# Hash products on four 32-column strips of the array, and normalised rows on ScalarE

## The chip, the cores and the metric

One core of a Trainium2 chip runs one program. The metric is the device time of one execution in microseconds; a run gives several executions and the median is quoted. One execution more is taken with the hardware profiler on, and the views below are all of that one.

## What is computed

Three layers run one after the other on 2 x 768 tokens of width 512. The first is attention with 8 heads of width 64 in which a query sees only the keys of its own hash bucket; the bucket is the sign pattern of six projections. The second mixes tokens by the real part of a two-dimensional Fourier transform, normalises each row and applies a feed-forward of width 2048. The third is a gated layer of width 1024.

```python
q_bits = (np.einsum('bhsd,dk->bhsk', q, proj) > 0)      # proj is 64 x 6; k_bits likewise
mask = q_bucket[:, :, :, None] == k_bucket[:, :, None, :]
scores = np.where(mask, scale * q @ k.T, -1e9)          # then softmax, then @ v
...
u = x + np.real(fft(fft(x, axis=1), axis=2))
un = (u - mu) / np.sqrt(var + 1e-06)                    # mu, var of each row of 512
y = u + np.maximum(un @ w_ch1, 0.0) @ w_ch2
...                                                     # gated layer: w_in, gelu, w_sg, w_out
```

## The kernel before, in words

**Tiling.** Attention is cut into 16 heads (2 batches of 8), two heads to a group (8 groups), and each head into 6 items of 128 queries. An item is a 128 x 768 score tile `s` on TensorE (L394), its row maximum on VectorE (L404), the exponential on ScalarE (L406), a split into high and low halves (L251 on ScalarE or L253 on GpSimd, then L258 on GpSimd), a transpose by DMA (L445), and the product with V (L462 to L464).

**The hash.** `prep_group` loads the two `x` tiles of a group; each has the 64 query rows over the 64 key rows, 768 tokens wide. For each half of the tokens (384) and each of the two heads one matmul in F32 (L311) multiplies `x` by `zp`, 128 x 24, so `z` holds 24 rows of projections, 6 for queries and 6 for keys of each head. One ScalarE instruction turns `z` into signs, `bits` (24 rows x 768 columns, F16, L280, in `to_bits`). For each head `prep_head` multiplies `bits` by a table of codes in two matmuls of 384 columns (L360) and `one_hot` writes the result behind the query and key rows (L287, L289). Scores of unlike buckets come out low in the score product itself. The first group's hash is at the head of the program; the others are spread over the items before their heads.

**The normalisation.** After the Fourier steps of a batch (`fft`), `norm` makes for each of 6 row blocks `un = (u - mu) * i` in F32 on VectorE (L640), a high half on ScalarE (L641), a low half on GpSimd (L642) and a transpose by DMA (L643), which gives `unT`, the operand of the feed-forward. In batch 0 the tiles `un` and `hl` share a ring of four buffers of the tag `k2` with the first feed-forward tiles. In batch 1 `un` has one buffer.

**What sets the order.** The program is written as merged streams: attention, weight decoding (the int64 view of the float64 weights is turned to F32 at L226 to L228, then split at L239 and L241), Fourier and feed-forward. Then `Order`, a list scheduler with a table of costs, plans all of it and fixes the order on each engine and of the DMA issues on SP. It plans several times: a rank that blends the start time of the best plan so far with the tail of each node, one plan for each entry of `BLEND`, and keeps the plan with the shortest planned time. Each engine then runs its instructions strictly in that order.

**The stages.** Items of batch 0 until about 143 us; Fourier of batch 0 between the items of batch 1; first feed-forward matmuls (L667, L688) at 232.5 us; the rest of batch 1's attention until 367 us under the feed-forward of batch 0; Fourier of batch 1; feed-forward of batch 1 until 546 us; the gated layer (L764, L787, L804) until the end.

Of the kernel before, what the change touches and what calls it, by code (L numbers as in the profile page):

```python
# [81 lines left out]


def _until(gen, cond):
    for _ in gen:
        if cond():
            return
# [16 lines left out]
class Kern:  # L104
    def __init__(self, tc, I, out):
        self.tc, self.nc, self.I, self.out = tc, tc.nc, I, out
        self.W = {}
        self.c2n, self.att_over = 0, False


# [43 lines left out]
    def setup(self, ctx):  # L154
# [122 lines left out]

    def to_bits(self, out, z):
        if BITS == "A":
            self.nc.scalar.activation(out, z, AF.Sign, bias=self.tiny[0:24])  # L280
        else:
            self.nc.vector.tensor_scalar(out=out, in0=z, scalar1=0.0, scalar2=None, op0=ALU.is_gt)

    def one_hot(self, eng, qo, ko, c):
# [8 lines left out]
    def prep_group(self, ap, vp, n, G):  # L293
# [10 lines left out]
        yield  # L304
        bits = self.bits[n % 2]
        to = bits[0:24].rearrange("p (a c) -> p a c", a=2)
        z = None if ZP[b] else self.ps.tile([P, 2, 512], F32, tag="s", name="z")
        for hf in range(2):
            zh = self.pp.tile([P, 512], F32, tag="p", name="z")[:, 0:HS] if ZP[b] else z[:, hf, 0:HS]
            for hl in range(GH):  # L310
                nc.tensor.matmul(zh[0:24], self.zp[:, hl, :], xs[hl][:, hf * HS:(hf + 1) * HS], start=hl == 0, stop=hl == GH - 1)  # L311
            if ZP[b]:
                self.to_bits(to[:, hf], zh[0:24])
        if not ZP[b]:
            self.to_bits(to, z[0:24, :, 0:HS])
        yield
# [23 lines left out]
    def prep_head(self, ap, n, hl, G):  # L340

        nc, I = self.nc, self.I
        b, g = divmod(n, NG)
        eng = ENG0 if n + hl == 0 else ENG[b]
        x = G["x"][hl]
        if GH * n + hl in FULL:
            q1, k1 = (ap.tile([P, S], F32, tag=nm, name=nm, bufs=SB) for nm in ("q1", "k1"))
            nc.sync.dma_start(out=q1[0:64], in_=I["qk"][b, GH * g + hl, 0:64])
            self.copy(eng["hi"], k1[0:64], x[64:128], SCALE)
            G[hl] = ((q1, k1),)  # L350
        else:
            G[hl] = self.stacks(ap, x, eng)
            q1, k1 = G[hl][0]
        yield
        bits = self.bits[n % 2]
        qo, ko = (y[64:128].rearrange("p (a c) -> p a c", a=2) for y in (q1, k1))
        ct = None if CP[b] else self.ps.tile([P, 2, 512], F32, tag="s", name="ct")
        for hf in range(2):
            c = self.pp.tile([P, 512], F32, tag="p", name="ct")[:, 0:HS] if CP[b] else ct[:, hf, 0:HS]
            nc.tensor.matmul(c, self.codes[:, hl, :], bits[:, hf * HS:(hf + 1) * HS], start=True, stop=True)  # L360
            if CP[b]:
                self.one_hot(eng["oh"], qo[:, hf], ko[:, hf], c)
        if not CP[b]:
            self.one_hot(eng["oh"], qo, ko, ct[:, :, 0:HS])
        yield
# [248 lines left out]
    def norm(self, fp, up, b, unT, mv, ts):  # L614
# [13 lines left out]
        nc.vector.reciprocal(s, i)  # L628
        nc.vector.tensor_tensor(out=self.tok[b][:, 2 * t0:2 * t0 + w], in0=rs, in1=s, op=ALU.mult)
        yield 0.9  # L630
        for t in ts:
# [5 lines left out]
            for n, X in enumerate((A, Bt)):  # L637
                un = fp.tile([P, DM], F32, tag="k2" if LN1[b] else "un", name="un", bufs=4 if LN1[b] else 1)
                hl = fp.tile([P, 2, DM], F16, tag="k2" if LN1[b] else "hl", name="hl", bufs=4 if LN1[b] else 2)
                nc.vector.tensor_scalar(out=un, in0=X, scalar1=mv[:, t, n, 0:1], scalar2=i[:, 2 * (t - t0) + n:2 * (t - t0) + n + 1], op0=ALU.subtract, op1=ALU.mult)  # L640
# [184 lines left out]
    def g_weights(self, wp):  # L825
# [7 lines left out]
        for nm, n, c in (("in", 4, 1024), ("out", 2, 1024), ("sg", 6, 768)):  # L833
            rs[nm] = [wp.tile([P, c], F32, tag=f"{nm}{j}", name=f"{nm}{j}") for j in range(n)]
            spare = sp["sg"] if nm == "sg" else (self.spare if nm == "out" else sp["in"])
            yield from self.weight(wp, nm, I["w_" + nm], rs[nm], spare, c, nc.sync)
        nc.vector.tensor_scalar(out=self.gB, in0=self.gB, scalar1=self.sc["sg"][0], scalar2=None, op0=ALU.mult)
        yield 0.5

    def build(self):  # L840
# [3 lines left out]
        with ExitStack() as ctx:  # L844
# [16 lines left out]
            def prep1():  # L861
                yield from self.weight(w1p, "w1a", I["w1"], r1[1:], r1[0], 1024, nc.sync, (0, 2, 4, 6))

            att = self.attention(ap, (ep0, ep1))
            p1 = prep1()
# [17 lines left out]
            def prep2():  # L883
                for half in HALVES:
                    if half == "b":
                        yield from self.weight(w2p, "w1b", I["w1"], r2[4:8], self.spare, 1024, nc.sync, (1, 3, 5, 7))
                    k = 8 * (half == "b")
                    bl = (4, 5, 6, 7) if k else (0, 1, 2, 3)
                    yield from self.weight(w2p, "w2" + half, I["w2"], r2[k:k + 4], self.spare, 1024, nc.sync, bl)
                    nc.vector.tensor_tensor(out=self.prod[half], in0=self.sc["w1" + half][0], in1=self.sc["w2" + half][0], op=ALU.mult)  # L890
                self.stage += 1

            def main0():
                yield from self.fft(fp0, 0, unT[0])
                self.stage += 1
                yield from self.ch(fp0, 0, unT[0], CH0, (("k2", 4),) * 4 + (("k1", 2),) * 2 + (("k3", 2),) * 2)

            def second():
# [7 lines left out]
                with tc.tile_pool(name="fft1", bufs=1) as fp:  # L906
                    yield from self.fft(fp, 1, unT[1], up)

# [13 lines left out]

            _run(_merge((self.ch(hp, 1, unT[1], CH1), 1.0), (side(), W3)))
            c_r.close()
# [14 lines left out]
class Order:  # L939
# [11 lines left out]
    def __init__(self, tc, room):  # L951
        self.tc, self.room = tc, room
        self.tiles = {t.name: t for t in tc.info.tiles}
# [31 lines left out]
    def cost(self, i, rd, wr):  # L985
# [3 lines left out]
        if e == "PE":  # L989
# [281 lines left out]
    def best(self):  # L1271
        self.rank = list(range(len(self.nodes)))
        self.slots()
        t, order = self.plan()
        found = t, order, [(n.start, n.end) for n in self.nodes]
        begin = [n.start for n in self.nodes]
        for f in self.BLEND:
            tail = self.tails()
            self.rank = [f * x - (1.0 - f) * y for x, y in zip(begin, tail)]
            t, order = self.plan()  # L1280
            if t < found[0]:
                found = t, order, [(n.start, n.end) for n in self.nodes]
                begin = [n.start for n in self.nodes]
        return found[1]

# [17 lines left out]
def _tables():  # L1303
# [21 lines left out]
    rl[0] = np.where(l % 2 == 0, 1.0, -1.0)  # L1325
    codes = np.zeros((P, GH, P), np.float16)
    sign = np.where((np.arange(64)[None, :] >> np.arange(NB)[:, None]) & 1, 1.0, -1.0)
# [4 lines left out]
    pops = np.zeros((P, 2), np.float32)  # L1332
    if BITS == "A":
        pop = np.full_like(pop, NB)
    pops[0:64, 0] = BIG * (1.0 - pop)
# [49 lines left out]
```

## Time and profile before

| | us |
|---|---|
| median of 3 runs | 695.46 |
| range of the runs | 695.41 to 697.05 |
| profiled execution | 692.43 |
| its span | 690.6 |
| mean granted clock of TensorE | 0.963 |

The profiled execution lies 3.03 us below the median, and 1.8 us of it lie outside the span. In the rows, PE is TensorE's matmuls, PEld its weight loads, DVE VectorE, ACT ScalarE, POOL GpSimd, SP the issuer of the DMAs. `L311` is line 311 of the kernel. A matmul's shown duration includes its way through the array, so the distance between two starts, not the duration, is what one costs in a full stream. An FP32 matmul stands as two records.

### The profile page before, as it was taken

What the parts mean: (1) busy time and instruction counts of PE and PEld (TensorE: products, weight loads), DVE (VectorE), ACT (ScalarE), POOL (GpSimd) and SP (SyncE); (2) the same over time, 40 slices, a digit from 0 to 9 for tenths busy, and PEclk for the clock granted to TensorE, in tenths of its full rate; (3) what the DMA queues carried; (4) which work ended last, traced back from release to release, by engine and by line L of the source; (5) the groups of instructions that cost most, each with busy time, mean ns of one, the idle gap of its engine ahead of it and who ended that gap; (6) DMA issues with size and microseconds to landing.
All of it is one profiled execution on the core that took longest, in us unless ns stands there. A gap on an engine that the chain in (4) does not pass through costs nothing.

```text
span 690.6 us, 12566 instructions
## 1 busy us (share of the span) xinstructions
PE 627.7 (91%) x4832; PEld 416.9 (60%) x4832; DVE 503.2 (73%) x1137; ACT 347.8 (50%) x540; POOL 232.3 (34%) x197
## 2 busy tenths in 40 slices
PE   4899988865986689999999999998999999999997
PEld 2586776844664467667777658666766444444443
DVE  7968675599799987889557289858563467876663
ACT  5899797866577574467442222324632143322100
POOL 3576645596477630445345032000000022111000
PEclk9999999985996799999999999999999999999999
DMA  8999979999999995786563025943000031211334
GB/s 325 265 163 198 202 176 201 199 245 279 249 209 232 225 220 174 184 184 115 108 107 110 1 36 122 257 126 103 31 1 0 1 58 36 32 31 31 67 86 122
DMA packets 184204, 95.19 MB, mean 138 GB/s; under 512 B 166544, under 2 KB 167312, under 8 KB 183632
## 3 DMA queue, kind: packets, MB, share of 16 engines
q1 hardware_dynamic: 183568, 94.25, 61.3%
q8 instruction: 38, 0.62, 0.4%
q10 hardware_dynamic: 576, 0.14, 0.1%
q14 instruction: 22, 0.18, 0.1%
HBM read 39.31 MB, written 3.15 MB: 61 GB/s over the span
## 4 chain that ended last, share of the span: by engine, by line
PE 44%; DVE 10%; DMA 5%; ACT 2%; POOL 1%; issue 1%; DVEq 0%; POOLq 0%; ACTq 0%
PE c L667 10%; PE c L688 9%; PE gi L764 9%; PE sg L787 7%; PE go L804 5%; DMA wide<-w_in 3%; DMA wide<-w 1%; PE y L549 1%; PE s L394 1%; DVE xu L692 1%; DVE w L241 1%; DVE h L676 1%; DVE nm L404 1%; DVE in L227 1%; DVE w L227 1%
## 5 line engine op out<-in xcount | busy, mean ns | idle before, releaser
L258 POOL TENSOR_TENSOR eh<-e,eh 128x768 f16<-128x768 f32 x80 | 138.5, 1735 | 103.1 <-ACT eh L251 100.8
L667 PE MATMUL c<-unT,w 128*128 128x256 f16 x1152 | 137.2, 277 | 4.8 <-DVE h L676 4.1
L688 PE MATMUL c<-w,h 128*128 128x512 f16 x576 | 131.7, 379 | 1.7 <-DVE xu L692 1.7
L667 PEld LDWEIGHTS <-w 128*128 128x128 f16 x1152 | 113.5, 99 | 27.9 <-issue 7.4
L394 PE MATMUL s<-k,q 128*128 128x384 f32 x384 | 100.1, 391 | 31.4 <-ACT e L406 18.2
L404 DVE TENSOR_REDUCE nm<-s 128x1 f32<-128x768 f32 x96 | 90.2, 949 | 32.7 <-PE s L394 31.4
L406 ACT ACTIVATE e<-s,nm 128x768 f32<-128x768 f32 x96 | 85.2, 896 | 40.2 <-DVE nm L404 28.1
L394 PEld LDWEIGHTS s<-k,q 128*128 128x128 f32 x384 | 69.4, 205 | 41.0 <-ACT e L406 21.7
L688 PEld LDWEIGHTS <-h 128*128 128x128 f16 x576 | 55.5, 98 | 60.9 <-issue 2.6
L780 POOL TENSOR_TENSOR vh<-gv,vh 128x512 f16<-128x512 f32 x12 | 13.9, 1156 | 195.5 <-ACT vh L779 195.5
L675 ACT ACTIVATE h<-c 128x256 f16<-128x256 f32 x96 | 35.0, 377 | 60.4 <-PE c L667 59.9
L676 DVE SCALAR_TENSOR_TENSOR h<-c,h 128x256 f16<-128x256 f32 x96 | 39.1, 418 | 34.3 <-ACT h L675 34.3
L462 PE MATMUL pav<-V,et 128*128 128x65 f16 x480 | 55.3, 199 | 7.4 <-DVE xu L471 4.1
L462 PEld LDWEIGHTS <-et 128*128 128x128 f16 x480 | 46.6, 103 | 16.4 <-issue 10.6
L463 PE MATMUL pav<-V,et 128*128 128x64 f16 x480 | 54.9, 198 | 0.0
L464 PE MATMUL pav<-V,et 128*128 128x65 f16 x480 | 54.8, 200 | 0.0
L764 PE MATMUL gi<-in,xT 128*128 128x512 f16 x216 | 50.5, 379 | 0.0
L764 PEld LDWEIGHTS <-xT 128*128 128x128 f16 x288 | 28.1, 98 | 35.0 <-issue 1.1
L463 PEld LDWEIGHTS <-et 128*128 128x128 f16 x480 | 46.6, 101 | 1.9 <-issue 0.7
L464 PEld LDWEIGHTS <-et 128*128 128x128 f16 x480 | 46.5, 101 | 0.0
L253 POOL TENSOR_SCALAR eh<-e 128x768 f16<-128x768 f32 x32 | 32.7, 1022 | 32.2 <-ACT e L406 25.6
L251 ACT ACTIVATE eh<-e 128x768 f16<-128x768 f32 x48 | 40.3, 839 | 3.0 <-DMA et<-eh 2.5
(221 smaller groups left out, 999.4 us busy)
## 6 DMA issues: line engine op xcount, KB each, us to landing
wide<-w SPq DMA_DIRECT2D x24, 512.0 KB, 4.5
x<-qk SPq DMA_DIRECT2D x16, 384.0 KB, 4.8
k<-q SPq DMA_DIRECT2D x28, 192.0 KB, 3.6
wide<-w SPq DMA_DIRECT2D x4, 1024.0 KB, 9.0
wide<-w_in SPq DMA_DIRECT2D x16, 256.0 KB, 3.1
vst<-v SPq DMA_DIRECT2D x8, 396.0 KB, 6.0
y<-ot SPq DMA_DIRECT2D x12, 256.0 KB, 2.3
q<-q SPq DMA_DIRECT2D x14, 192.0 KB, 4.5
```

Source lines behind the costliest of these rows:

```text
L258: (self.nc.vector if eng == "D" else self.nc.gpsimd).tensor_tensor(out=out, in0=a, in1=b, op=ALU.subtract)
L394: nc.tensor.matmul(s[:, hf, 0:HS], q[:, qs], k[:, hf * HS:(hf + 1) * HS], start=n == 0, stop=n == len(pairs) - 1)
L404: nc.vector.tensor_reduce(nm, x["s"], axis=AX.XY, op=ALU.max, negate=True)
L406: nc.scalar.activation(e.rearrange("p (a c) -> p a c", a=2), x["s"], AF.Exp, bias=nm)
L462: nc.tensor.matmul(pv[:, qt, 0:65], et[:, kb, :], V[:, hl, kb, 64:129], start=kb == 0, stop=False)
L463: nc.tensor.matmul(pv[:, qt, 0:64], et[:, kb, :], V[:, hl, kb, 0:64], start=False, stop=False)
L464: nc.tensor.matmul(pv[:, qt, 0:65], et[:, NT + kb, :], V[:, hl, kb, 64:129], start=False, stop=kb == NT - 1)
L667: nc.tensor.matmul(ps[:, 0:step], w1[kc][:, a, fo], uT[:, 4 * u + kc, o * P:o * P + step], start=m == 0, stop=m == 11)
L676: nc.vector.scalar_tensor_tensor(out=hh[:, 1, :], in0=ps[:, 0:step], scalar=0.0, in1=hh[:, 0, :], op0=ALU.max, op1=ALU.subtract)
L688: nc.tensor.matmul(ps, hs[n, half, f][:, a, j * P:(j + 1) * P], wv[:, w, :], start=f + m == 0, stop=f == NF - 1 and m == 2)
L764: nc.tensor.matmul(ps, xT[:, 4 * a + kc, :], w_in[kc][:, w, half * DM:(half + 1) * DM], start=n == 0, stop=n == 11)
L787: nc.tensor.matmul(ps, w_sg[kt][:, w, t * P:(t + 1) * P], vh[b][:, kt, a, :], start=n == 0, stop=n == 17)
```

## The change

- **Hash products.** The 768 tokens are cut in four quarters of 192. `zp` gets 32 columns for each head in place of 24. For each head and quarter one matmul of 192 columns goes to a strip of 32 columns of the array, so that `z` is 128 rows by 192 columns in place of 24 by 768. The sign instruction reads and writes 128 x 192.
- **Codes.** Since the signs of quarter g lie on rows 32g to 32g + 23, the table of codes stands four times, once for each strip, the other rows zero. It is zeroed by GpSimd and filled by four DMAs from ScalarE's queue, where one was. The product with the codes is four matmuls of 192 columns for each head. The zeroing of the two `bits` tiles goes.
- **Rows.** `un` is made on ScalarE as `i * u + g` with `g = -mu * i`; `g` is one small VectorE instruction more in each call of `norm` (one call in batch 0, three in batch 1).
- **Order.** The planner prices an F32 matmul with 32 output rows at a quarter, blends with 0.75 six times in place of five different values, and shifts the rank of the stream that loads and decodes `w_out` by -15 us. Naming of the streams is only for that.

```diff
+UN = ('A', 'A')
-BITS = 'A'
+SQ = S // 4
...
-        self.codes = cp.tile([P, GH, P], F16, tag="codes", name="codes")
+        self.codes = cp.tile([P, 4, GH, P], F16, tag="codes", name="codes")
+        nc.gpsimd.memset(self.codes, 0.0)
...
-        nc.scalar.dma_start(out=self.codes, in_=I["codes"])
+        for g in range(4):
+            nc.scalar.dma_start(out=self.codes[32 * g:32 * g + 2 * GH * NB, g], in_=I["codes"])
...
-        self.zp = cp.tile([P, GH, 2 * GH * NB], F32, tag="zp", name="zp")
+        self.zp = cp.tile([P, GH, 32], F32, tag="zp", name="zp")
...
-            t = cp.tile([P, S], F16, tag=f"bits{i}", name=f"bits{i}")
-            nc.gpsimd.memset(t, 0.0)
+            t = cp.tile([P, SQ], F16, tag=f"bits{i}", name=f"bits{i}")
...
-        for hf in range(2):
-            zh = self.pp.tile([P, 512], F32, tag="p", name="z")[:, 0:HS] if ZP[b] else z[:, hf, 0:HS]
-            for hl in range(GH):
-                nc.tensor.matmul(zh[0:24], self.zp[:, hl, :], xs[hl][:, hf * HS:(hf + 1) * HS], start=hl == 0, stop=hl == GH - 1)
...
-            self.to_bits(to, z[0:24, :, 0:HS])
+            z = self.ps.tile([P, 2, 512], F32, tag="s", name="z")[:, 0, 0:SQ]
+        for hl in range(GH):
+            for c in range(4):
+                nc.tensor.matmul(
+                    z[32 * c:32 * c + 32], self.zp[:, hl], xs[hl][:, c * SQ:(c + 1) * SQ],
+                    start=hl == 0, stop=hl == GH - 1, tile_position=(0, 32 * c),
+                )
+        nc.scalar.activation(self.bits[n % 2], z, AF.Sign, bias=self.tiny)
...
-            nc.tensor.matmul(c, self.codes[:, hl, :], bits[:, hf * HS:(hf + 1) * HS], start=True, stop=True)
+            for a in range(2):
+                nc.tensor.matmul(c[:, a * SQ:(a + 1) * SQ], self.codes[:, 2 * hf + a, hl], bits, start=True, stop=True)
...
+        if UN[b] == "A":
+            g = fp.tile([P, w], F32, tag="lnm", name="lnm", bufs=1 if LN1[b] else 2)
+            nc.vector.scalar_tensor_tensor(
+                out=g.rearrange("p (a c) -> p a c", c=2), in0=mv[:, t0:ts[-1] + 1, :, 0], scalar=-1.0,
+                in1=i.rearrange("p (a c) -> p a c", c=2), op0=ALU.mult, op1=ALU.mult,
+            )
...
+                if UN[b] == "A":
+                    nc.scalar.activation(un, X, AF.Identity, scale=i[:, c], bias=g[:, c])
...
+    SHIFT = {"out": -15.0}
-    BLEND = (0.0, 0.25, 0.5, 0.75, 0.9)
+    BLEND = (0.75,) * 6
...
-                return x * (2 if i.is_transpose else 4) / 2400 + 0.0065
+                return x * (2 if i.is_transpose else 1 if wr[0][2] - wr[0][1] == 32 else 4) / 2400 + 0.0065
...
-            self.rank = [f * x - (1.0 - f) * y for x, y in zip(begin, tail)]
+            self.rank = [f * x - (1.0 - f) * y + z for x, y, z in zip(begin, tail, self.shift)]
```

## Rows read from the trace of the kernel before

**Rows 1.** Stages: busy us of PE, PEld, DVE, ACT, POOL (instructions), granted clock, DMA share.
```profile
34.00:138.00 104.00, 94.92 (x1013) 79.84 (x1012) 70.49 (x111) 90.73 (x123) 64.09 (x51) 0.98 0.99 190
138.00:207.00 69.00, 52.47 (x525) 38.81 (x524) 60.67 (x97) 45.96 (x68) 47.89 (x41) 0.85 1.09 245
207.00:258.00 51.00, 35.71 (x314) 28.11 (x315) 47.61 (x87) 35.68 (x51) 31.45 (x24) 0.77 1.09 227
258.00:690.00 432.00, 422.68 (x2861) 256.22 (x2859) 294.58 (x802) 152.21 (x268) 73.56 (x57) 1.00 0.37 85
546.00:690.00 144.00, 140.02 (x648) 63.23 (x647) 95.74 (x314) 35.10 (x53) 13.88 (x12) 1.00 0.26 55
```

**Rows 2.** Chain that ended last, pieces: start, length in us, what.
```profile
253.49 1.24 DVE w L227
...
262.54 2.69 PE z L311 x8
...
546.75 36.42 PE gi L764 x168
```

**Rows 3.** Groups of instructions: count, busy us, mean ns of one, idle before.
```profile
L311 PE MATMUL z<-x,zp 128*24 128x384 f32 x64 | 23.8, 515 | 7.4 <-DVE zp L172 4.6 <-ACT e L406 1.4 <-DMA x<-qk 1.4
L280 ACT ACTIVATE bits<-z,tiny 24x768 f16<-24x768 f32 x8 | 7.1, 885 | 2.7 <-PE z L311 2.7
L675 ACT ACTIVATE h<-c 128x256 f16<-128x256 f32 x96 | 35.0, 377 | 60.4 <-PE c L667 59.9
```

**Rows 4.** Weight loads of one group's hash products: start, length in us.
```profile
263.13 0.10 PEld L311 LDWEIGHTS z<-x,zp 128*24 128x24 f32 x1 [0.22 <-issue]
263.45 0.10 PEld L311 LDWEIGHTS z<-x,zp 128*24 128x24 f32 x1 [0.22 <-issue]
```

**Rows 5.** Matmuls of lines 463 and 464: start, length in us.
```profile
27.05 0.19 PE L463 MATMUL pav<-V,et 128*128 128x64 f16 x1
27.08 0.20 PE L464 MATMUL pav<-V,et 128*128 128x65 f16 x1
```

**Rows 6.** First 12 us: ScalarE's queue, its first instruction, GpSimd's zeroing.
```profile
1.16 0.46 ACTq L163 DMA_DIRECT2D codes<-codes  x1
...
5.59 0.84 ACT L251 ACTIVATE k<-q 64x768 fp32r<-64x768 f32 x1 [1.69 <-DVE q L255]
...
L176 POOL MEMSET bits<- 128x768 f16 x2 | 1.4, 737 | 0.3 <-POOLq L1373 0.3
```

**Rows 7.** Row normalisation of batch 0 on VectorE, and GpSimd beside it.
```profile
213.08 0.58 DVE L640 TENSOR_SCALAR un<-xu,mv,ln 128x512 f32<-128x512 f32 x1
...
216.89 1.79 DVE L640 TENSOR_SCALAR un<-xu,mv,ln 128x512 f32<-128x512 f32 x1
...
216.74 3.43 POOL L258 TENSOR_TENSOR eh<-e,eh 128x768 f16<-128x768 f32 x2
```

**Rows 8.** Line 640, VectorE's busy us (x instructions), granted clock, in both batches.
```profile
213.00:236.00 23.00, 6.59 (x6) 0.65 1.12 214
396.00:424.00 28.00, 3.27 (x6) 1.00 0.30 48
```

**Rows 9.** ScalarE instructions of 128x512: with a scale by row, without.
```profile
L731 ACT ACTIVATE ghl<-xu,x_i 128x512 f16<-128x512 f32 x12 | 8.5, 715 | 11.1 <-DVE x_i L132 5.5 <-DMA xT<-ghl 4.1 <-DVE x_s L131 1.5
...
L641 ACT ACTIVATE hl<-un 128x512 f16<-128x512 f32 x12 | 7.5, 627 | 23.1 <-DVE lnp L118 12.4 <-DVE un L640 10.7
```

**Rows 10.** Waits until 138 us: total us, times, longest.
```profile
DVE nm L404 <- PE s L394: 21.1, 24, 2.5
```

**Rows 11.** Score products, four records, before and after the clock rose.
```profile
223.54 1.63 PE L394 MATMUL s<-k,q 128*128 128x384 f32 x4
226.26 0.95 PE L394 MATMUL s<-k,q 128*128 128x384 f32 x4
```

**Rows 12.** A feed-forward matmul that waited, and the first decoding of w_out.
```profile
468.44 1.46 PE L688 MATMUL c<-w,h 128*128 128x512 f16 x6 [1.66 <-DVE xu L692]
...
470.86 0.28 DVE L226 TENSOR_SCALAR out<-wide 128x256 int32<-128x256 int32 x1
```

More of the change, by code (lines that the diff above doesn't have):

```diff
@@ L81, in _merge, with _named @@
         yield 0.0
+def _named(kern, name, gen):
+    while True:
+        at = len(kern.nc.cur_bb.bb.instructions)
+        try:
+            x = next(gen)
+        except StopIteration:
+            kern.name(at, name)
+            return
+        kern.name(at, name)
+        yield x
 def _until(gen, cond):
@@ L108, in __init__, with name @@
         self.c2n, self.att_over = 0, False
+        self.stream = {}
+    def name(self, at, name):
+        if name == "att":
+            name = "att%d" % (getattr(self, "item", 0) >= H * NT)
+        for i in self.nc.cur_bb.bb.instructions[at:]:
+            self.stream.setdefault(i.name, name)
     def rsqrt(self, pool, x, n, t=None):
@@ L276, in stacks @@
         return (q1, k1), (q2, k2)
[L278 to L282, printed above, removed]
     def one_hot(self, eng, qo, ko, c):
@@ L304, in prep_group @@
         yield
-        bits = self.bits[n % 2]
-        to = bits[0:24].rearrange("p (a c) -> p a c", a=2)
-        z = None if ZP[b] else self.ps.tile([P, 2, 512], F32, tag="s", name="z")
-        for hf in range(2):
-            zh = self.pp.tile([P, 512], F32, tag="p", name="z")[:, 0:HS] if ZP[b] else z[:, hf, 0:HS]
-            for hl in range(GH):
-                nc.tensor.matmul(zh[0:24], self.zp[:, hl, :], xs[hl][:, hf * HS:(hf + 1) * HS], start=hl == 0, stop=hl == GH - 1)
-            if ZP[b]:
-                self.to_bits(to[:, hf], zh[0:24])
-        if not ZP[b]:
-            self.to_bits(to, z[0:24, :, 0:HS])
+        if ZP[b]:
+            z = self.pp.tile([P, 512], F32, tag="p", name="z")[:, 0:SQ]
+        else:
+            z = self.ps.tile([P, 2, 512], F32, tag="s", name="z")[:, 0, 0:SQ]
[6 more added lines that the diff above has]
+        nc.scalar.activation(self.bits[n % 2], z, AF.Sign, bias=self.tiny)
         yield
@@ L835, in g_weights @@
             spare = sp["sg"] if nm == "sg" else (self.spare if nm == "out" else sp["in"])
-            yield from self.weight(wp, nm, I["w_" + nm], rs[nm], spare, c, nc.sync)
+            yield from _named(self, nm, self.weight(wp, nm, I["w_" + nm], rs[nm], spare, c, nc.sync))
         nc.vector.tensor_scalar(out=self.gB, in0=self.gB, scalar1=self.sc["sg"][0], scalar2=None, op0=ALU.mult)
@@ L861, in prep1 @@
             def prep1():
-                yield from self.weight(w1p, "w1a", I["w1"], r1[1:], r1[0], 1024, nc.sync, (0, 2, 4, 6))
-            att = self.attention(ap, (ep0, ep1))
+                yield from _named(self, "w1a", self.weight(w1p, "w1a", I["w1"], r1[1:], r1[0], 1024, nc.sync, (0, 2, 4, 6)))
+            att = _named(self, "att", self.attention(ap, (ep0, ep1)))
             p1 = prep1()
@@ L885, in prep2 @@
                     if half == "b":
-                        yield from self.weight(w2p, "w1b", I["w1"], r2[4:8], self.spare, 1024, nc.sync, (1, 3, 5, 7))
+                        yield from _named(self, "w1b", self.weight(w2p, "w1b", I["w1"], r2[4:8], self.spare, 1024, nc.sync, (1, 3, 5, 7)))
                     k = 8 * (half == "b")
                     bl = (4, 5, 6, 7) if k else (0, 1, 2, 3)
-                    yield from self.weight(w2p, "w2" + half, I["w2"], r2[k:k + 4], self.spare, 1024, nc.sync, bl)
+                    yield from _named(self, "w2" + half, self.weight(w2p, "w2" + half, I["w2"], r2[k:k + 4], self.spare, 1024, nc.sync, bl))
                     nc.vector.tensor_tensor(out=self.prod[half], in0=self.sc["w1" + half][0], in1=self.sc["w2" + half][0], op=ALU.mult)
@@ L893, in main0 @@
             def main0():
-                yield from self.fft(fp0, 0, unT[0])
+                yield from _named(self, "fft0", self.fft(fp0, 0, unT[0]))
                 self.stage += 1
-                yield from self.ch(fp0, 0, unT[0], CH0, (("k2", 4),) * 4 + (("k1", 2),) * 2 + (("k3", 2),) * 2)
+                yield from _named(self, "ch0", self.ch(fp0, 0, unT[0], CH0, (("k2", 4),) * 4 + (("k1", 2),) * 2 + (("k3", 2),) * 2))
             def second():
@@ L906, in second @@
                 with tc.tile_pool(name="fft1", bufs=1) as fp:
-                    yield from self.fft(fp, 1, unT[1], up)
+                    yield from _named(self, "fft1", self.fft(fp, 1, unT[1], up))
             _run(_merge((second(), lambda: W1[self.stage]), (main0(), 1.0), (prep2(), lambda: W2[self.stage])))
@@ L921, in side @@
                     yield 2.0
-            _run(_merge((self.ch(hp, 1, unT[1], CH1), 1.0), (side(), W3)))
+            _run(_merge((_named(self, "ch1", self.ch(hp, 1, unT[1], CH1)), 1.0), (side(), W3)))
             c_r.close()
@@ L945, with __init__ @@
     GAP = {"DVE": 0.19, "POOL": 0.13}
+    SHIFT = {"out": -15.0}
     LOOK, OVER = 12, 0.3
     WINDOW = 3.413
-    BLEND = (0.0, 0.25, 0.5, 0.75, 0.9)
+    BLEND = (0.75,) * 6
     LAP = {"PE": 0.0, "DVE": 0.075, "ACT": 0.1, "POOL": 0.045, "SP": 0.0}
-    def __init__(self, tc, room):
-        self.tc, self.room = tc, room
+    def __init__(self, tc, room, stream):
+        self.tc, self.room, self.stream = tc, room, stream
         self.tiles = {t.name: t for t in tc.info.tiles}
@@ L1273, in best @@
         self.slots()
+        self.shift = [self.SHIFT.get(self.stream.get(n.ins[0].name), 0.0) for n in self.nodes]
         t, order = self.plan()
@@ L1283, in best @@
                 begin = [n.start for n in self.nodes]
+        self.value, self.begin = found[0], begin
         return found[1]
@@ L1325, in _tables @@
     rl[0] = np.where(l % 2 == 0, 1.0, -1.0)
-    codes = np.zeros((P, GH, P), np.float16)
+    codes = np.zeros((2 * GH * NB, GH, P), np.float16)
     sign = np.where((np.arange(64)[None, :] >> np.arange(NB)[:, None]) & 1, 1.0, -1.0)
@@ L1332, in _tables @@
     pops = np.zeros((P, 2), np.float32)
-    if BITS == "A":
-        pop = np.full_like(pop, NB)
+    pop = np.full_like(pop, NB)
     pops[0:64, 0] = BIG * (1.0 - pop)
@@ L1377 @@
         room = nc.sbuf_top - nc.sbuf_base
-        Kern(tc, I, out).build()
-        Order(tc, room).apply()
+        kern = Kern(tc, I, out)
+        kern.build()
+        Order(tc, room, kern.stream).apply()
     r = _launch(nc, [arrays], core_ids=[0])
```

4 lines of the change are left out of this document (3 added, 1 removed).

## Prediction

> **What bounds the kernel now.** I read the table of stages first [rows 1], because the share of busy time over the whole span hides that the stages differ. From 258 us to the end TensorE is busy in 422.68 of 432 us at full clock: it is the bound there, with 9.3 us of idle time in all. Before 258 us nothing of the kind holds. In 34 to 138 us ScalarE carries 90.73 of 104 us (87%) and TensorE's 94.92 us are long records, not a full stream. In 207 to 258 us VectorE is busy 47.61 of 51 us (93%) while TensorE has 35.71 us at a granted clock of 0.77. The chain of work that ended last agrees [rows 2]: before 257 us it runs through ScalarE and VectorE, behind that nearly all of its long pieces are matmuls; one group's hash products lie on it, 2.69 us from 262.54 us. So I ask of each part which of the two halves it helps: up to 258 us VectorE and ScalarE, behind that TensorE alone.
>
> **Hash products.** They are 64 records, eight for each group [rows 3]. Weight loads of one group start 0.32 us apart [rows 4], so one record of 384 columns costs 0.32 us in the stream and the eight records of a group 2.57 us. Eight groups are 20.6 us. The change makes 16 records of 192 columns, 0.16 us each if the cost goes by columns. Their cost in strips isn't in this trace, so I bound it. One after the other they cost 2.57 us again; four abreast 0.64 us. If each must also show its weight load of 0.10 us [rows 4], 16 x 0.26 = 4.2 us. I take a value between: the two records of one matmul fall on the same strip and follow each other, and only the second runs beside the first of the next strip, which gives 9 x 0.16 = 1.44 us. It is nearest to what rows 4 show, a stream in issue order with loads hidden under the matmul before. A group then saves 1.1 us of TensorE (bounds -1.6 and +1.9).
>
> Only one group lies in TensorE's half, at 262.5 us: **term A, 1.1 us** (-1.6 to +1.9). The other seven lie before 258 us, where TensorE's time isn't the bound; what they give comes in through ScalarE.
>
> A record lasts 0.515 us in the mean [rows 3], 0.19 us longer than its distance to the next, the way through the array. The Trainium skill ("TensorEngine Tiling (Array Packing)", Key Properties) says that a change of tiling mode drains the engine, which speaks against this change: two changes in each group. By that rule, an estimate with the 0.19 us for each drain, the one group on the chain would save 0.7 in place of 1.1 us; no run here shows it yet.
>
> **Signs.** One instruction of 24 x 768 takes 0.885 us [rows 3]. It goes by columns, so 128 x 192 should be near the 0.377 us of the 128 x 256 row; I take 0.35 us, 0.53 us saved in each group. Four groups (1 to 4) have their hash between 23 and 144 us, in the stretch that ScalarE paces: **term B, 4 x 0.53 = 2.1 us**. If ScalarE's spare 13% swallows it, 0; if the shorter hash products, which the score products queue behind, count there in full too, 4 x (1.1 + 0.53) = 6.5 us. I take the middle row because ScalarE's is the fullest.
>
> **Codes.** 32 matmuls of 384 columns become 64 of 192. Columns are the same; 32 more weight loads are hidden, since matmuls with a load each run 0.03 us apart at lines 462 to 464 [rows 5] and these stream 0.08 us. Uncovered, 32 x 0.03 = 1 us over all, none of it in one place. Nothing.
>
> **Start.** Three more DMA issues of 0.46 us on ScalarE's queue, 1.4 us, and the first of them waits for the zeroing of the codes: 1024 columns in place of the 768 of one `bits` tile at 0.737 us, so 0.98 us from about 0.8 us, which ends 0.6 us behind the present issue at 1.16 us. The other constants' issues, the table load and ScalarE's first instruction queue behind it. That instruction waits 1.69 us for VectorE today [rows 6]; 2.0 us of delay leave 0.3 us, and the shorter first hash and signs give back 0.5 us. Nothing; without that wait it would cost up to 2.0 us.
>
> **Rows on ScalarE.** In batch 0 six `un` instructions take 6.59 us of VectorE, in batch 1 six take 3.27 us [rows 8]. A long one, 1.79 us, runs beside GpSimd work; a short one takes 0.58 us [rows 7]. On ScalarE each should be near the 0.715 us of the row with a scale by row, more than the 0.627 us without [rows 9]: 6 x 0.715 = 4.3 us, in a stretch where ScalarE has 15 us idle of 51 [rows 1]. There each queues behind exponentials and casts, but its high half follows on the same engine without a change of engine. VectorE gains at least six short ones, 6 x 0.55 = 3.3 us, less 0.2 us for `g`; the 3.3 us of waiting beside GpSimd may only move to the next VectorE instruction. **Term C, 3.1 us** (0 if ScalarE's queue or the DMA transposes set the pace, 6.4 if all of it counts). Batch 1's lie at 396 to 424 us under the full TensorE; were that cover gone, the chain of un, high half, low half would differ by 0.715 - 0.55 = 0.17 us for each block. Nothing.
>
> **Order.** Ranks, blends and the shift of `w_out` change the order on every engine. The trace can only bound it: behind 258 us there are 9.3 us of idle time [rows 1], of which the last 4 are the end of the program, so 5.3 us at most to gain there. To lose: below. I take 0.
>
> **Sum.** 1.1 + 2.1 + 3.1 = 6.3 us. The profiled execution takes 692.43 us; 686.1 us follow for its like. It lies 3.03 us below the median of the runs, so against the median 695.46 - 6.3 = 689.2 us.
>
> **The rivals.**
>
> *Larger gain.* The strips run four abreast and the plan fills the TensorE time with other work: 8 groups x 1.9 = 15.4 us freed, of which the one in the full half and half of the rest count, 1.9 + 6.7, and 6.4 us of VectorE: 15.0 us, 680.5 us. For it: feed-forward work stands ready behind 232 us, and VectorE is full. Against: before 143 us TensorE has no other work, and three of the groups lie there.
>
> *Hidden.* ScalarE's slack, the DMA share of 0.99 to 1.09 up to 258 us [rows 1] and GpSimd set the pace, and only term A counts: 694.4 us. For it: three resources are close together there. Against: VectorE has no idle stretch when the first feed-forward matmul becomes possible.
>
> *Slower, by the clock.* The granted clock before 138 us is 0.98, and 0.65 in 213 to 236 us, where TensorE had idled more before [rows 1, 8]; each is a mean of the two levels, 1.2 and 2.4 GHz. The hash products are solid work in that stretch. If shorter ones let the clock drop there as it does behind 207 us, a score product takes 1.63 in place of 0.95 us [rows 11]. VectorE waited for one 24 times in 138 us [rows 10]: 24 x 0.68 = 16.3 us lost, less the 6.3: 705.5 us if it falls for all of the stretch. It decides from 40% of the score products at half clock, where the loss equals the gain. Against: the other matmuls there are untouched.
>
> *Slower, by the order.* `w_out`'s decoding starts at 470.86 us; 15 us earlier it stands before the eviction that a feed-forward matmul already waited 1.66 us for [rows 12]. Six such waits, 10 us, would make it 699.2 us.
>
> **How the numbers follow.** The forecast has 0.53, the larger gain 0.20, hidden 0.13, slower 0.14 (clock 0.06, order 0.08). The range leaves out a tenth on each side: half of the larger gain below 680 us, most of the slower ones above 698 us. Some 0.3%, 2.1 us, is what a measurement can tell from no change: faster 0.73, same 0.13, slower 0.14.
>
> **What would show it.** In the profile of the changed kernel: the start of one hash record to the next, and one group's eight products from first to last (0.6, 1.4, 2.6 or over 4 us); the sign instruction near 0.35 us; `un` on ScalarE near 0.7 us; VectorE's busy time in the 50 us before the first full feed-forward stretch; the start of that stretch earlier than 257 us by about 5 us (terms B and C), and the rest from there to the end shorter by 1 us. Wrong if that start doesn't move, if the granted clock before 138 us falls, or if idle time of TensorE behind 258 us changes by more than a few us, which would be the order's work.

## The result and the profile after

| | before | changed |
|---|---|---|
| median of the runs, us | 695.43 (4 runs, 695.17 to 697.05) | 685.12 (4 runs, 682.66 to 689.58) |
| ratio, 95% interval | | 0.9849 (0.9802 to 0.9895) |
| profiled execution, us | 692.43 | 686.57 |
| its span, us | 690.6 | 684.8 |
| mean granted clock | 0.963 | 0.960 |

The change makes the kernel faster by 10.3 us, 1.5%. 689.2 us was forecast. The executions of the changed kernel lie 7 us apart, those of the kernel before 2 us here and 5 to 8 us in the later sets of runs; a second profiled execution of the same changed program, in the run e5 below, had a span of 677.1 us. So landmarks of one profile are good for some us and no better, and what follows rests on ratios with intervals wherever it can.

Three moments cut the program into stretches: the first Fourier instruction on GpSimd, `fo` (batch 0's items are done), the first feed-forward matmul, and the first matmul `gi<-in` of the gated layer, written `gi` below (0.6 us behind the very first matmul into the tile `gi`). First the kernel before, then the changed one, by these stretches; columns as in [rows 1].

```profile
0.00:144.20 144.20, 120.89 (x1170) 96.58 (x1171) 104.87 (x159) 118.02 (x161) 83.96 (x83) 0.98 0.99 217
144.20:232.50 88.30, 64.10 (x632) 48.35 (x630) 80.64 (x141) 59.94 (x86) 62.06 (x49) 0.79 1.10 240
232.50:547.40 314.90, 303.38 (x2389) 208.98 (x2389) 223.31 (x525) 134.74 (x242) 72.38 (x55) 0.99 0.48 110
547.40:690.60 143.20, 139.38 (x646) 62.95 (x644) 94.38 (x313) 35.10 (x53) 13.88 (x12) 1.00 0.26 56
```

```profile
0.00:147.30 147.30, 116.01 (x1244) 98.89 (x1244) 104.17 (x160) 116.41 (x162) 81.76 (x80) 0.97 0.99 213
147.30:227.90 80.60, 60.00 (x575) 46.26 (x575) 74.64 (x140) 57.30 (x86) 58.05 (x46) 0.75 1.07 240
227.90:541.70 313.80, 303.09 (x2466) 211.69 (x2465) 218.12 (x519) 142.54 (x253) 77.87 (x58) 0.99 0.52 116
541.70:684.80 143.10, 139.41 (x646) 62.99 (x644) 94.43 (x313) 35.11 (x53) 13.91 (x12) 1.00 0.24 56
```

The first stretch is 3.1 us longer, not shorter. The second is 7.7 us shorter, with VectorE as full as before (93% against 91%). The third is 1.1 us shorter; the gated layer is unchanged, as it must be.

The parts themselves, in groups of the changed kernel's profile (columns as in [rows 3]):

```profile
L327 PE MATMUL z<-x,zp 128*32 128x192 f32 x128 | 8.4, 381 | 6.2 <-DVE zp L195 4.6 <-ACT e L423 1.0 <-DMA x<-qk 0.6
L331 ACT ACTIVATE bits<-z,tiny 128x192 f16<-128x192 f32 x8 | 3.3, 417 | 1.4 <-PE z L327 1.3
L665 ACT ACTIVATE un<-xu,lnm,ln 128x512 f32<-128x512 f32 x12 | 9.7, 809 | 15.6 <-DVE lnp L139 8.9 <-POOL hl L669 3.9 <-DVE lnm L649 2.8
```

TensorE is busy 8.4 us with hash products where [rows 3] have 23.8 us. The signs take 0.417 us each in place of 0.885 us, the rows 0.809 us each on ScalarE. One group, in order of time (start and length in us; a weight-load row, two of matmuls, then the next weight load):

```profile
264.64 0.48 PEld L327 LDWEIGHTS z<-x,zp 128*32 128x32 f32 x16
264.65 0.86 PE L327 MATMUL z<-x,zp 128*32 128x192 f32 x16
265.44 2.76 PE L715 MATMUL c<-w,h 128*128 128x512 f16 x12
265.43 2.49 PEld L715 LDWEIGHTS <-h 128*128 128x128 f16 x13 [0.30 <-issue]
```

From the first hash product to the next other matmul 0.79 us pass, where [rows 2] have 2.69 us: 1.9 us of TensorE is freed in a group. The sixteen records start within 0.53 us (0.86 us less the 0.33 us of the last). Behind the strips the weight loads pause for 0.30 us before the next 128-column load. Whatever the change between strips and full array costs is counted in the 0.79 us. The Trainium skill ("TensorEngine Tiling (Array Packing)", Key Properties) says that a change of tiling mode drains the engine. The trace doesn't show whether the pause is that, for in the kernel before, whose code names no strips, the loads behind the group pause longer, 0.63 us:

```profile
265.16 2.52 PEld L667 LDWEIGHTS <-w 128*128 128x128 f16 x24 [0.63 <-issue]
```

**The start.** Here the change loses. ScalarE's queue at the head of the changed kernel:

```profile
2.16 7.07 ACTq L186 DMA_DIRECT2D codes<-codes  x4
9.26 1.28 ACT L273 ACT_TABLE_LOAD   x1 [9.26 <-DMA codes<-codes]
10.55 0.84 ACT L273 ACTIVATE k<-q 64x768 fp32r<-64x768 f32 x1
```

And the chain of work that ended last, which in this profile reaches back to the start:

```profile
1.67 7.23 DMA ident<-ident
...
8.92 5.48 DMA codes<-codes
...
14.45 0.35 PE ct L377
```

The four issues take 7.07 us in place of 4 x 0.46 us. In the program each of the last three waits for a semaphore of an earlier DMA, and the chain shows which one held the fourth: the table `ident`, 7.23 us after its issue. ScalarE's first instruction starts at 10.55 us where it started at 5.59 us [rows 6], the fourth part of the table lands at 14.4 us, and the first score product starts at 16.7 us where it started at 12.9 us. In the second execution of the same program (e5) `ident` landed sooner and held ScalarE for less:

```profile
1.64 3.87 DMA ident<-ident
```

There the four issues take 3.70 us and the first score product starts at 13.3 us. So this loss changes from execution to execution: 13.3 to 16.7 us in the six profiles with four code DMAs (changed, e1, e3, e5, e6, e9), 12.9 to 13.3 us in the six with the old table.

### The profile page after: what moved, and what is told of

Read it like the earlier page. It is cut to its first block, busy times and chain, and to the rows that moved or that the text cites. A ratio compares the mean times of both kernels' runs of the same rounds, so it can differ in the third digit from the quotient of the medians.

```text
span 684.8 us, 12786 instructions
## 1 busy us (share of the span) xinstructions
PE 618.5 (90%) x4928; PEld 419.8 (61%) x4928; DVE 491.4 (72%) x1129; ACT 351.4 (51%) x552; POOL 231.6 (34%) x196
## 4 chain that ended last, share of the span: by engine, by line
PE 58%; DVE 18%; DMA 11%; ACT 5%; POOL 3%; issue 3%; SPq 0%; ACTq 0%; DVEq 0%; POOLq 0%
PE c L715 14%; PE c L694 10%; PE gi L791 9%; PE sg L814 7%; PE s L411 5%; PE go L831 5%; DVE nm L421 3%; DMA et<-eh 3%; DMA wide<-w 2%; PE y L566 2%; DMA wide<-w_in 2%; DVE w L250 2%; DVE w L249 2%; POOL eh L280 2%; PE po L474 2%
## 5 line engine op out<-in xcount | busy, mean ns | idle before, releaser
L280 POOL TENSOR_TENSOR eh<-e,eh 128x768 f16<-128x768 f32 x80 | 140.8, 1762 | 103.6 <-ACT eh L273 101.6
L694 PE MATMUL c<-unT,w 128*128 128x256 f16 x1152 | 134.5, 274 | 6.8 <-DVE h L703 6.7
L411 PE MATMUL s<-k,q 128*128 128x384 f32 x384 | 105.0, 403 | 26.1 <-ACT e L423 14.3
L411 PEld LDWEIGHTS s<-k,q 128*128 128x128 f32 x384 | 71.7, 212 | 35.8 <-ACT e L423 18.8
L479 PE MATMUL pav<-V,et 128*128 128x65 f16 x480 | 56.4, 200 | 5.5 <-DMA et<-eh 2.5
L481 PE MATMUL pav<-V,et 128*128 128x65 f16 x480 | 55.7, 201 | 0.0
L703 DVE SCALAR_TENSOR_TENSOR h<-c,h 128x256 f16<-128x256 f32 x96 | 38.1, 415 | 23.8 <-ACT h L702 23.7
L275 POOL TENSOR_SCALAR eh<-e 128x768 f16<-128x768 f32 x32 | 30.0, 938 | 34.6 <-ACT e L423 32.0
```

Source lines behind the costliest of these rows:

```text
L280: (self.nc.vector if eng == "D" else self.nc.gpsimd).tensor_tensor(out=out, in0=a, in1=b, op=ALU.subtract)
L411: nc.tensor.matmul(s[:, hf, 0:HS], q[:, qs], k[:, hf * HS:(hf + 1) * HS], start=n == 0, stop=n == len(pairs) - 1)
L479: nc.tensor.matmul(pv[:, qt, 0:65], et[:, kb, :], V[:, hl, kb, 64:129], start=kb == 0, stop=False)
L481: nc.tensor.matmul(pv[:, qt, 0:65], et[:, NT + kb, :], V[:, hl, kb, 64:129], start=False, stop=kb == NT - 1)
L694: nc.tensor.matmul(ps[:, 0:step], w1[kc][:, a, fo], uT[:, 4 * u + kc, o * P:o * P + step], start=m == 0, stop=m == 11)
```

## The experiments

All ratios are to the kernel before on the same chip, with their 95% interval. "Hash" is strips, signs and code tables; "rows" is `un` on ScalarE; "order" is the six blends of 0.75 with the shift of `w_out`.

| run | hash | rows | order | median us | ratio | interval |
|---|---|---|---|---|---|---|
| changed | new | new | new | 685.12 | 0.9849 | 0.9802 to 0.9895 |
| e5_after_again | new | new | new | 681.47 | 0.9811 | 0.9768 to 0.9853 |
| e1_rows_back | new | old | new | 681.76 | 0.9829 | 0.9796 to 0.9863 |
| e2_hash_back | old | new | new | 687.61 | 0.9904 | 0.9873 to 0.9935 |
| e3_order_back | new | new | old | 685.42 | 0.9879 | 0.9848 to 0.9910 |
| e6_hash_alone | new | old | old | 682.77 | 0.9828 | 0.9792 to 0.9864 |
| e7_rows_alone | old | new | old | 695.37 | 1.0003 | 0.9978 to 1.0028 |
| e8_order_alone | old | old | new | 686.44 | 0.9862 | 0.9825 to 0.9899 |
| e9_strips_in_turn | new, other turn | old | old | 683.87 | 0.9833 | 0.9797 to 0.9868 |
| e10_price_alone | old | old | old, hash priced low | 701.43 | 1.0088 | 1.0054 to 1.0122 |
| e11_no_blends | old | old | one plan, no blend | 689.59 | 0.9911 | 0.9879 to 0.9944 |
| e4_one_table | new, one table | new | new | 682.57 | 0.9834 | 0.9807 to 0.9861 |
| e12_best | new, one table | old | new | 680.52 | 0.9786 | 0.9752 to 0.9820 |

Theory: the gain is the sum of the parts' own work, as the prediction has it. Rival: the parts make the list scheduler find another order, and the order is the gain.

**One part put back.** First the changed kernel with one part undone.

e1_rows_back:
```diff
-UN = ('A', 'A')
+UN = ('D', 'D')
```


> The changed kernel with the normalised rows made on VectorE again; hash products, codes and order rules stay. If term C is what the rows on ScalarE bring, this loses about 3 us against the changed kernel (some 688 us). If the rows bring nothing because the stretch from the end of batch 0's items (147.3 us) to the first row instruction (209.3 us) was shortened by the order and the hash, it stays within 1 us (684 to 686 us). The new plan that the list scheduler makes can move it by a few us either way.

e2_hash_back (the old lines of the diff for `zp`, `z`, `bits` and `codes`):
```diff
-                    z[32 * c:32 * c + 32], self.zp[:, hl], xs[hl][:, c * SQ:(c + 1) * SQ],
+                nc.tensor.matmul(z[0:24, hf, 0:HS], self.zp[:, hl, :], xs[hl][:, hf * HS:(hf + 1) * HS], ...)
```


> The changed kernel with the old hash: 24-column products of 384 tokens in one stream, signs 24 rows high, one table of codes by one DMA. Rows on ScalarE and order rules stay. If the strips and the shorter signs carry the gain, this loses 4 to 8 us (689 to 693 us) in spite of a start that is some 4 us quicker, because the first score product waits for the four code DMAs in the changed kernel (16.7 us against 12.9 us). If the order carries it, the quicker start shows and it is as fast or faster (680 to 685 us).

e3_order_back:
```diff
-    SHIFT = {"out": -15.0}
-    BLEND = (0.75,) * 6
+    SHIFT = {}
+    BLEND = (0.0, 0.25, 0.5, 0.75, 0.9)
```


> The changed kernel with the old five blends and no shift of w_out; hash strips, signs and rows on ScalarE stay. If the stretch from the end of batch 0's items to the first row instruction was shortened by 7 us by the order, this loses about that (690 to 693 us). If hash and rows carry the gain, it stays near 685 us.

Without the new rows the kernel is as fast (0.9829; the two runs of the changed kernel gave 0.9849 and 0.9811). With the hash put back it keeps 0.9904, with the order put back 0.9879: each of hash and order can be taken away and most of the gain, or half of it, stays. Parts that add up don't behave so.

**One part alone.** The changed kernel was run again beside the three parts taken singly, each the reverse of the edits above, made on the kernel before.

> The changed kernel itself, on the same chip as the three kernels that take one part alone, so that their differences can be formed without a change of chip. 685 us, 0.985 of the kernel before.

> The kernel before with the hash strips, the signs 128 rows high and the four code DMAs, and nothing else: rows on VectorE, old blends, no shift. The changed kernel without rows is as fast as with them, and without its order rules it loses little, so if the hash is the main part it alone gives most of the gain: 686 to 688 us, in spite of a start some 3 us late. If the parts need each other (an order that uses the freed time), it gives 2 us or less (692 to 694 us).

> The kernel before with the normalised rows on ScalarE and nothing else. Term C of the prediction would give 3 us (691 us); the run with rows put back says nothing or a loss (694 to 697 us), because a row instruction lasts 0.81 us on ScalarE where 0.72 us was forecast, and two ScalarE instructions then stand one behind the other in each block.

> The kernel before with six blends of 0.75 and the shift of w_out, and nothing else. If the order by itself shortened the stretch from batch 0's last item to the first feed-forward matmul, it gives 4 to 7 us (687 to 690 us). If it only helps together with the hash, it gives 0 to 2 us (692 to 695 us).

Hash alone gives 0.9828, order alone 0.9862, rows alone 1.0003; all together 0.9811. The two that work give 1.7 and 1.4%, and all three together 1.9% (1.5% in the first runs). The rows are worth nothing that can be measured: an interval of 0.25% to either side. Order alone is the telling run, since in it no instruction does other work than before: 9 us come from the order by itself.

**The same work in other orders.** e10 and e11 change only the planner, on the kernel before.

e10_price_alone:
```diff
-                return x * (2 if i.is_transpose else 4) / 2400 + 0.0065
+                return x * (2 if i.is_transpose else 1 if wr[0][2] - wr[0][1] == 24 else 4) / 2400 + 0.0065
```


> The kernel before with every instruction as it was; only the planner believes that a hash product costs a quarter of its true price, as the changed kernel's planner does. The order on the engines changes, the work doesn't. If a new order by itself makes a gain like that of the hash alone, this comes out well below the kernel before (682 to 690 us). If the strips' own time is the gain, it stays at 694 us or loses.

e11_no_blends:
```diff
-    BLEND = (0.0, 0.25, 0.5, 0.75, 0.9)
+    BLEND = ()
```


> The kernel before with every instruction as it was, planned once in the order of the program, without any of the five blends. Its order has 72 score rows taken on VectorE before the first feed-forward eviction, 18 of them of batch 1, where the kernel before has 77 (23 of batch 1); the hash alone has 71. If the number of items put ahead of the feed-forward sets the time, this gains several us (685 to 690 us), some 3 us for each item that is moved from the stretch paced by VectorE to the one paced by TensorE, less what the poorer plan loses elsewhere. If not, it is at 694 us or slower, as its planned time is longer.

One plan is 0.9% slower than the kernel before, the other 0.9% faster; with e8 the same work spans 1.0088 to 0.9862, some 16 us. That a plain plan without any blend beats the chosen one says that the planned time by which the scheduler picks doesn't rank real times at this distance.

What the order does can be read from the stretches. Below, from one profiled execution each, the start of the first feed-forward matmul, TensorE's busy and idle time from there to `gi`, and the number of score rows (L404 of the kernel before) that start between `fo` and that matmul (54 of the 96 start ahead of `fo` in every run):

| kernel | `fo` us | first feed-forward us | TensorE busy to `gi` us | idle us | score rows between |
|---|---|---|---|---|---|
| before | 144.2 | 232.5 | 303.4 | 11.5 | 21 |
| changed | 147.3 | 227.9 | 303.1 | 10.7 | 19 |
| e5, changed again | 144.3 | 224.6 | 301.2 | 8.2 | 19 |
| e1 rows back | 147.3 | 224.4 | 308.9 | 7.2 | 17 |
| e2 hash back | 142.6 | 226.6 | 305.7 | 10.2 | 19 |
| e3 order back | 144.7 | 232.9 | 300.4 | 7.8 | 22 |
| e6 hash alone | 148.5 | 222.9 | 307.6 | 7.2 | 16 |
| e7 rows alone | 147.0 | 231.5 | 305.3 | 13.5 | 20 |
| e8 order alone | 142.8 | 229.3 | 304.0 | 7.0 | 20 |
| e10 price alone | 148.1 | 236.5 | 304.5 | 14.4 | 20 |
| e11 no blends | 147.7 | 225.4 | 308.4 | 11.7 | 17 |

Two of its rows in the profile, the second and third stretch of e6 and of e11:

```profile
148.50:222.90 74.40, 53.06 (x541) 40.19 (x541) 68.42 (x129) 48.12 (x75) 50.75 (x45) 0.79 1.08 236
222.90:537.70 314.80, 307.56 (x2515) 214.69 (x2515) 235.18 (x538) 146.75 (x255) 81.26 (x61) 0.99 0.52 122
```

```profile
147.70:225.40 77.70, 54.33 (x541) 38.95 (x539) 72.38 (x133) 50.93 (x75) 55.15 (x44) 0.85 1.02 238
225.40:545.50 320.10, 308.38 (x2477) 213.59 (x2477) 233.24 (x533) 144.09 (x251) 77.91 (x59) 0.99 0.51 117
```

These times come from one execution each. The two profiles of the changed program, one plan, differ by 3.3 us in the start of the feed-forward, 1.9 us in busy and 2.5 us in idle time, so a split of a run's gain is no finer than that.

*Which items stand ahead.* Between `fo` and the first feed-forward matmul VectorE is 90 to 96% busy in all of these, and a plan with fewer items of batch 1 there has a shorter stretch. The stretch also holds Fourier steps and normalisation of batch 0, so its length by item (88.3 / 21 = 4.2 us) isn't what one more item costs; that is read from the difference between plans. In e11, the same work as before, four items fewer make it 10.6 us shorter, 2.7 us each. But `fo` comes 3.5 us later, so the feed-forward starts 7.1 us earlier, and behind its start the four items raise TensorE's busy time by 5.0 us (25 score rows against 21): 2.1 us are left, some 0.5 us for each item. In e6 the feed-forward starts 9.6 us earlier and the five items more behind it (26) raise the busy time by 4.2 us, with one cheaper group of hash products among it. So placing items behind the feed-forward's start brings little in e11 and at most 5.4 us in e6, where the hash's own work changed too. And e3 gains without it: its feed-forward starts as late as before, at 232.9 us, with one item more ahead, and `gi` still comes 6.3 us earlier, by 3.0 us less busy and 3.7 us less idle time.

*How long TensorE stands idle behind that start:* 7.0 to 14.4 us. Of the 7.1 us by which `gi` starts earlier in e8 it is 4.5, with 3.2 from the earlier start and 0.6 us more of busy time against it; of the 8.0 us by which `gi` starts later in e10 it is 2.9. Where these waits sit differs from plan to plan, and none of the runs takes a single one out.

*TensorE's clock.* It isn't the same behind that start. The first 25 us of it, before, changed, e5 (columns as in [rows 1]):

```profile
232.50:257.50 25.00, 19.57 (x171) 15.25 (x171) 23.11 (x35) 17.13 (x27) 12.69 (x10) 0.85 1.07 230
227.90:252.90 25.00, 22.97 (x228) 18.92 (x227) 18.19 (x30) 16.68 (x28) 15.18 (x10) 0.93 1.08 242
224.60:249.60 25.00, 23.07 (x243) 19.45 (x243) 19.71 (x33) 16.68 (x29) 15.09 (x10) 1.00 1.08 244
```

A mean of 0.85 is some 7.5 us of the 25 at the lower of the two levels, where a score product takes 1.63 us in place of 0.95 us [rows 11]; by that, an estimate, 3 us are lost there before, about half of it in the changed kernel and nothing in e5. In e8 the figure is 0.96, in e10 0.80. So a few of the microseconds between plans, and most of the 1.9 us of busy time between the two executions of the changed kernel, may be the clock's. No run takes it apart from the order.

**Is it the strips' own time?** e9 keeps e6's order on every engine and was to make only the hash products dearer:
```diff
-        for hl in range(GH):
-            for c in range(4):
+        for c in range(4):
+            for hl in range(GH):
```


> The kernel with the hash strips alone, with exactly its order on every engine, but inside each group the eight hash products go strip by strip (both heads on one strip, then the next strip) in place of head by head. Each strip then gets four records behind each other. If a strip works its own records off in turn, a group takes about 13 x 0.16 = 2.1 us in place of the 0.53 us that the changed kernel showed, and only the hash products' time differs. If that time is what gave the 12 us, most of it is lost (some 690 us, 0.993 or more of the kernel before); if the new order gave it, the loss is 1 to 3 us (684 to 686 us).

It didn't make them dearer. A group, start and length:

```profile
263.97 0.88 PE L327 MATMUL z<-x,zp 128*32 128x192 f32 x16
```

0.88 us against 0.86 us, so the run tells nothing of what the strips' time is worth. It tells two other things. Four records behind each other on one strip cost no more than four on four strips. And the same plan in another set of runs gives 0.9833 against 0.9828: the ratio of this plan repeats to 0.05% (and TensorE's busy and idle time behind the feed-forward's start to 0.1 us), while plans differ by 1% and more. The changed kernel's own plan repeated less well, 0.9849 and 0.9811. How much of the hash alone's 12 us is the 1.9 us freed in each group and how much the order that its price led to stays open. With the new order in both, the hash is worth 0.9904 against 0.9811 and 0.9849, some 4 to 6 us, and there too the plans differ.

**The start mended.** One table for all strips, one DMA, no zeroing:
```diff
-        nc.gpsimd.memset(self.codes, 0.0)
-        for g in range(4):
-            nc.scalar.dma_start(out=self.codes[32 * g:32 * g + 2 * GH * NB, g], in_=I["codes"])
+        nc.scalar.dma_start(out=self.codes, in_=I["codes"])      # codes is now 128 x 4 x 2 x 128
```


> The changed kernel with the table of codes laid out for all four strips in memory and read by one DMA of 256 KB from ScalarE's queue, with no zeroing by GpSimd. In the changed kernel ScalarE's queue is held by the issues of the code DMAs until 9.26 us and the last of them lands at 14.4 us; the first score product starts at 16.7 us where it started at 12.9 us before. If that delay goes straight through to the end, this wins 3 to 4 us (681 to 682 us). If slack behind the start swallows it, it stays at 685 us.

e12_best is the same with `UN = ('D', 'D')`.

> The changed kernel with the rows on VectorE again and one code table by one DMA. The rows were worth nothing alone, and the one table takes 4 to 6 us off the first score product. If the start goes through, 677 to 680 us (0.976 to 0.979 of the kernel before); if the changed kernel's own order has swallowed it, 681 to 682 us (0.982).

ScalarE's queue at the start of e4:

```profile
1.16 0.45 ACTq L184 DMA_DIRECT2D codes<-codes  x1
...
2.61 1.28 ACT L271 ACT_TABLE_LOAD   x1 [2.61 <-issue]
5.29 0.84 ACT L271 ACTIVATE k<-q 64x768 fp32r<-64x768 f32 x1 [1.40 <-DVE q L275]
```

The mechanism is as told: 256 KB by one issue land in 4.5 us (4.4 us in e12), and the first score product starts at 10.9 us in both runs, where the changed kernel has 16.7 and 13.3 us. `fo` follows at 140.2 and 141.7 us, 3 to 7 us earlier. At the end e4 stands at 0.9834, between the changed kernel's 0.9811 and 0.9849, which is no gain, and e12 at 0.9786 beside 0.9829 of e1, 0.43% better with intervals that overlap. So the earlier start is shown, that it reaches the end is not. e12 has the lowest ratio of all, but its interval overlaps that of the changed kernel; it isn't shown to be faster.

## Why the prediction was right, and where it was not

The direction was right, the time lies in the range, and the size is 10.3 us against 6.3. That it came out near is in good part luck: terms that brought little or nothing stood in the sum, and the order, which alone is worth 9 us, stood at nothing. So the terms have to be judged one by one.

- **What bounds what.** Right. Behind the first feed-forward matmul TensorE is the bound in every profile (95 to 98% busy), ahead of it VectorE, and `gi` to the end is 143.0 to 143.3 us in all of them. The landmark was not: what was to come 5 us earlier is the start of TensorE's full stretch, at 257 us, by terms B and C. The first matmuls of that stretch, with the wait that ends before them, in the kernel before and the changed one:

```profile
257.15 1.47 PE L667 MATMUL c<-unT,w 128*128 128x256 f16 x12 [1.38 <-DVE h L676]
234.11 2.17 PE L694 MATMUL c<-unT,w 128*128 128x256 f16 x15 [2.03 <-DVE h L703]
```

  The stretch begins 23 us earlier, and what follows takes 17 us longer (450.7 us against 433.4 us) where 1 us less was forecast: work moved from one side of it to the other, which a sum of savings on either side can't show. The first feed-forward matmul came 4.6 us earlier in the profile.
- **Term A, hash products.** The row taken was the wrong end: records of one strip were assumed to wait for each other, 1.44 us for a group. A group takes 0.53 us from first start to last and 0.79 us to the next matmul, so it frees 1.9 us, the upper bound. The group behind 258 us has gone from the chain of the changed kernel.
- **Term B, signs.** 0.417 us where 0.35 us was put, 0.47 us saved in place of 0.53 us. The step that failed is that what ScalarE saves shortens batch 0's items: its busy time to `fo` fell from 118.0 to 116.4 us, but from the first score product to `fo` they took 131.3 us before (12.9 to 144.2) and 130.6 us (16.7 to 147.3) and 131.0 us (13.3 to 144.3) after. That is 0.3 to 0.7 us, not 2.1, and even so much can't be put down to the signs: with the old hash and other orders the same stretch took 129.5 us (e8) and 135.2 us (e10).
- **Start.** Put at nothing, with 2.0 us of delay counted (1.4 us of issues, 0.6 us of zeroing) and hidden behind a wait of 1.69 us; the profiled loss was 3.8 us at the first score product, and 0.4 us in e5. What failed is that only the issues' own time and the zeroing were priced. That an issue can wait for an earlier DMA to land, and the table load and all of ScalarE behind it, was not asked, although [rows 6] show what stands behind it in the queue.
- **Term C, rows.** 3.1 us forecast, nothing measured (e7 1.0003, e1 within the spread of the changed kernel). The duration was mis-sized: 0.809 us for each, 0.715 us forecast. The Trainium skill ("ScalarE: Activation LUTs", What ACT_TABLE_LOAD costs) gives 186 ns and 0.833 ns for each column, and some 93 ns for every operand that is a column of its own; `un` has two, so an estimate by that page is 0.80 us for 512 columns, and the trace agrees with 0.809 us. But 0.1 us isn't what undid the term. In e7 the stretch from `fo` to the first feed-forward matmul is 3.8 us shorter, with one item fewer in it, but `fo` comes 2.8 us later, and behind the start TensorE is busy 1.9 us and idle 2.0 us longer. So the stretch that the prediction looked at did get shorter, and the plan gave it back at both ends; how much of the 3.8 us is the rows' and how much the item's stays open.
- **Order.** Put at nothing, with 5.3 us as the most to gain behind 258 us. That is the term that failed most: order alone gives 0.9862, 9 us. The bound looked only at TensorE's idle time behind 258 us. In e8's profile 4.5 of the 7.1 us do come from less idle time behind the feed-forward's start, 232.5 us before; but the order also moved that start by 3.2 us, which the bound left out, and within the bound 0 was taken for no better reason than that the trace can't say more. Whether the six blends or the shift of `w_out` made it no run tells, since e8 has both.
- **The rivals.** The granted clock hardly moved in batch 0's items (0.97 in the changed kernel's first stretch, 0.98 before), so the slower rival by the clock is out. The rival by the order named the right part with the wrong sign here, and its mechanism didn't come about: `w_out`'s decoding starts at 465.2 us in place of 470.9 us, 5.7 us earlier, just as `gi` does. That an order can cost as much e10 shows, 1.0088, though by another way, since it doesn't shift `w_out`. Of the larger gain the first condition came true, strips that run abreast; its time, 680.5 us, is where e12 and three of e5's six executions came out (678.9 to 680.3 us), which is a likeness of numbers and no proof of its mechanism.

## What to carry to other kernels

Where a list scheduler orders everything, a change of cost or work is two changes, and the new plan can weigh more than the work: here the same instructions span 16 us over four plans. Price the order by its own runs (the new planner on the old work, the old planner on the new work) before crediting a saving. And count for every DMA that is added to an engine's queue what its issue may wait for and what stands behind it, not the issue time alone.

## What the runs showed of the hardware that was not expected

FP32 products of 128 rows by 32 columns, 192 columns each, started 0.035 us apart in a row of sixteen (0.53 us over 15 steps), a tenth of the 0.32 us of a 24-column product of 384 columns in the full array, and the whole group cost 0.79 us to the next matmul where the eight records of the old group cost 2.69 us. It made no difference whether neighbours in the row shared a strip (0.88 us for the group) or not (0.86 us). A DMA issue on ScalarE's queue waited for an earlier DMA to land, which took 7.23 us from its issue in one execution and 3.87 us in another of the same program, and ScalarE's table load and first instruction stood behind it. On ScalarE a sign of 128 x 192 took 0.417 us where a ReLU of 128 x 256 without a bias column took 0.377 us [rows 3], longer for fewer columns.
